# Sending the q transposes of four batches through the DMA crossbar instead of TensorE, and issuing the next batch's loads after the stores

## The chip, the cores and the metric

The kernel runs on one core of one Trainium2 chip. The time is the device time of one execution in microseconds (us); lower is better. Engines are named as the profile names them: PE is TensorE's matrix multiplication and PEld its weight loads, DVE is VectorE, ACT is ScalarE, POOL is GpSimd, SP is the engine that issues most of the DMA transfers. A transfer that an engine has issued runs on the 16 DMA engines, and is waited for by semaphore.

## The reference: what is computed

Sliding window attention for 8 batches of 8 heads, 576 positions and 64 elements a head, followed by a layer norm and a two-layer MLP with a residual. All inputs and the output are float32.

```python
# q, k, v: (8, 8, 576, 64); window = 64
scores = matmul(q, k.transpose(0, 1, 3, 2)) / sqrt(64)
rel = pos[:, None] - pos[None, :]
scores = where((rel >= 0) & (rel < window), scores, -1e9)
attn = softmax(scores, axis=-1)
x = matmul(attn, v)                        # heads side by side: (8, 576, 512)
xn = (x - mean(x)) / sqrt(var(x) + 1e-6) * g_ln
out = x + relu(xn @ w_ch1) @ w_ch2         # 512 -> 2048 -> 512
```

## The kernel before, in words

Positions 0 to 511 of a batch are one group of 512 tokens; the 64 last positions of all eight batches (the tails) make a ninth group. The outer loop, `for g in range(NGRP)`, runs the MLP of group `g`. While it does so, the same turn of the loop also carries the attention of group `g + 1` and the preparation of q, k and v of batch `g + 2`. In this text a turn is one pass of that loop.

The order of the work is written out by hand. `mlp_units` returns the MLP as a list of units, 30 of them from `g` = 2 on: 16 calls of `l1` (one 128 wide slice of the hidden layer, four 512 column matmuls, `hps`, and a relu on ScalarE into `hrT`), and then 14 calls of `stage`, two for each of seven products of a Strassen-like second layer (banks `pA`, `pB`, `pC`). `at(i, f, ...)` puts a step into slot `i`, which is emitted after unit `i`; a slot number that is too large means the last slot, after the last unit. Every engine, and every DMA queue, works through its own instructions in the order in which they were emitted. A step that waits therefore holds up what was emitted behind it on the same engine.

Slots 17 to 28 of a turn hold the preparation of batch `n = g + 2`, and these are the steps that matter here:

- `load_qk` (line 82) lets SP load q and k in two halves, each one transfer of 512 KB; from batch 2 on, each partition receives four successive positions, so that a run is 1 KB. `load_v` (line 135) loads v in four transfers of 256 KB. Loads of batch `n + 1` stand in slots 17, 18 and 23 of the turn before the one that casts them. Turn 1 loads batch 4 in slots 25, 26 and 28.
- `cast_qk` (line 120) converts a half of q and then the same half of k to float16 on GpSimd (line 126), in slots 11 and 16. GpSimd also carries `z_step` (line 306), the normalisation of a block of 128 tokens of group `g + 1`, in slots 2, 7, 12 and 17.
- `t_main` (line 211) brings a half of q or k into the layout with the head's elements on the partitions: eight 128x128 transposes on TensorE (line 216) into a PSUM tile `tp`, and one copy of 128x1024 into `qkT`, on ScalarE in these turns (line 207). The copy also puts the positions back into order. There are four such steps per batch, in slots 17 (q, first half), 19 (k, first half), 21 (q, second half) and 25 (k, second half).
- `s_mm` (line 240) computes the scores of two windows of 64 positions: 16 matmuls (line 263), with k as the weights and 64 columns of q as the moving operand, into two PSUM tiles `sc`; then two Exp instructions (line 266) on ScalarE write the float16 tile `pt`. `s_mm` of block 0 of batch `n` stands in slot 27, blocks 1 to 3 follow in slots 2, 7 and 12 of the next turn. `s_mask` (line 268) multiplies by the mask on VectorE.
- `b_step` (line 275) multiplies by v on TensorE (`xps`) and normalises on VectorE (line 297) into `x_norm`, a pool of four buffers of two blocks each; `z_step` follows it, and `zt_step` (line 321) transposes `z` on TensorE (line 328, tile `ztp`), six slots after the `b_step`.
- `stage` adds the second layer's products to `x_norm` and stores it: blocks 2 and 3 first, then blocks 0 and 1, at the end of the turn.
- `load_tail` (line 97) loads q, k and v of two batches' tails in six transfers, in slot 5 of turns 2, 4 and 6.

The transposes' PSUM tiles alternate between two banks (`t_tile`) up to slot 20 and share one after that.

Of the kernel before, what the change touches and what calls it, by code (L numbers as in the profile page):

```python
# [10 lines left out]
FP32 = mybir.dt.float32  # L11
# [3 lines left out]
AF = mybir.ActivationFunctionType  # L15
# [5 lines left out]
def kernel(  # L21
# [10 lines left out]
    nc = tc.nc  # L32
    B, H, S, D = q.shape
    DM = H * D
    HID = 4 * DM
    SM = 512
    NGRP = B + 1
    NKC = DM // 128
    NHC = HID // 128
    NHP = H // 2  # L40
    EPS = 1e-6
    scale = 1.0 / (D ** 0.5)

    p_const = ctx.enter_context(tc.tile_pool(name="pconst", bufs=1))
# [5 lines left out]
    p_xn = ctx.enter_context(tc.tile_pool(name="pxn", bufs=4))  # L50
# [21 lines left out]
    def t_tile(shape, name):  # L72
        i = 0 if tbank["shared"] else tbank["n"] % 2
        tbank["n"] = i + 1
        return ps_t.tile(shape, FP16, tag=f"t{i}", name=name)
# [3 lines left out]
    qkT, vA, vB, pts = {}, {}, {}, {}  # L79
    x_norm, zT, mvg, zsd, rstd = {}, {}, {}, {}, {}  # L80
# [36 lines left out]
        nc.gpsimd.tensor_copy(out=k16, in_=tk)  # L117
        nc.gpsimd.tensor_copy(out=vt[:, :, :, 0:D], in_=tv)

    def cast_qk(b, half):  # L120
        for x in range(2):
            t = qk32.pop((b, x, half))
            dst = p_in.tile([128, 8, 2, D], FP16, tag=f"qk16_{x}", name=f"qk16_{x}_{b}_{half}")
            qk16[(b, x, half)] = dst
            j = 2 if b < 2 else 4
            nc.gpsimd.tensor_copy(  # L126
                out=dst[:, :].rearrange("p (a j) e d -> p a e j d", j=j),
                in_=t[:, :].rearrange("p (a e j d) -> p a e j d", e=2, j=j, d=D),
            )
# [71 lines left out]
    def alloc_qkT(b):  # L201
        qkT[b] = [p_qkt.tile([128, NHP, SM + 64 * x], FP16, tag=f"qkT{x}", name=f"qkT{x}_{b}") for x in range(2)]
        nc.gpsimd.memset(qkT[b][1][:, :, 0:64], 0.0)

    def evac(x, out, in_):
        if x == 0:
            nc.scalar.copy(out=out, in_=in_)  # L207
        else:
            nc.vector.tensor_copy(out=out, in_=in_)

    def t_main(b, x, half, eng=None):
        src = qk16.pop((b, x, half))
        j = 2 if b < 2 else 4
        tp = t_tile([128, 8, 128], f"tp_{b}_{x}_{half}")
        for i in range(8):
            nc.tensor.transpose(out=tp[:, i, :], in_=src[:, i], identity=ident16)  # L216
        if b < 2:
            c0 = 64 * x + 256 * half
            dst = qkT[b][x][:, :, c0:c0 + 256]
        else:  # L220
            dst = qkT[b][x][:, 2 * half:2 * half + 2, 64 * x:64 * x + 512]
        evac(x if eng is None else eng, dst.rearrange("c h (p j) -> c h p j", j=j),
             tp[:, :].rearrange("c (h j) p -> c h p j", j=j))
# [16 lines left out]
    def s_mm(g, j, pe_mask=False):  # L240
        sc = [ps_s.tile([128, NHP, 2, 64], FP32, tag="sc", name=f"sc_{g}_{j}_{par}") for par in range(2)]
        pt = p_pt.tile([128, 2, NHP, 2, 64], FP16, tag="pt", name=f"pt_{g}_{j}")
        pts[(g, j)] = pt
        if pe_mask:
            m = mbias[:, :]
            mb = bass.AP(tensor=m.tensor, offset=m.offset, ap=[m.ap[0], [0, NHP * 2], m.ap[1]])
            for par in range(2):
                nc.tensor.matmul(
                    out=sc[par][:, :].rearrange("p h w i -> p (h w) i"), lhsT=ident16, rhs=mb,
                    start=True, stop=False, skip_group_check=True,  # L250
                )
        for hp in range(NHP):
            for iw in range(2):
                for par in range(2):
                    rows = slice(64 * par, 64 * par + 64)
                    if g == NGRP - 1:
                        lhsT = tailT[j][1][rows, iw, hp, :]
                        rhs = tailT[j][0][rows, hp, 64 * iw:64 * iw + 64]
                    else:
                        w = 2 * j + iw  # L260
                        lhsT = qkT[g][1][rows, hp, 64 * w:64 * w + 128]
                        rhs = qkT[g][0][rows, hp, 64 * w:64 * w + 64]
                    nc.tensor.matmul(out=sc[par][:, hp, iw, :], lhsT=lhsT, rhs=rhs,  # L263
                                     start=not pe_mask, stop=True, skip_group_check=pe_mask)
        for par in range(2):
            nc.scalar.activation(out=pt[:, par], in_=sc[par], func=AF.Exp, bias=0.0, scale=scale)  # L266

    def s_mask(g, j):
        pt = pts[(g, j)]
# [5 lines left out]
    def b_step(g, kb):  # L275
        kblk = f"{g}_{kb}"
        sfx, nb = ("r", 2) if g == NGRP - 1 else ("", None)
        if kb % 2 == 0:
            x_norm[(g, kb // 2)] = p_xn.tile([128, 2, DM], FP32, tag="xn" + sfx, name=f"xn_{g}_{kb // 2}", bufs=nb)
        xv = x_norm[(g, kb // 2)][:, kb % 2, :]  # L280
        xn = xv.rearrange("p (h d) -> p h d", h=H)
        xps = ps_x.tile([128, H, 128], FP32, tag="xps", name=f"xps_{kblk}")
        pt = pts.pop((g, kb))
        for h in range(H):
            par, hp = h % 2, h // 2
            for r in range(2):
                if sfx:
                    rhs = vT[kb][:, r, h, :]
                else:
                    rhs = (vA if r else vB)[g][:, kb, h, :]  # L290
                nc.tensor.matmul(out=xps[64 * r:64 * r + 64, h, :D + 1], lhsT=pt[:, par, hp, r, :], rhs=rhs,  # L291
                                 start=True, stop=True)
        rcp = p_blk.tile([128, H], FP32, tag="rcp", name=f"rcp_{kblk}")
        nc.vector.reciprocal(out=rcp, in_=xps[:, :, D])  # L294
        rcp_b = bass.AP(tensor=rcp.tensor, offset=rcp[:, :].offset,
                        ap=[rcp[:, :].ap[0], rcp[:, :].ap[1], [0, D]])
        nc.vector.tensor_tensor(out=xn, in0=xps[:, :, 0:D], in1=rcp_b, op=ALU.mult)  # L297
        stats = p_blk.tile([128, nc.vector.BN_STATS_DIM], FP32, tag="stats", name=f"stats_{kblk}")
        nc.vector.bn_stats(out=stats, in_=xv)  # L299
        if g not in mvg:  # L300
            mvg[g] = p_grp.tile([128, 4, 2], FP32, tag="mvg" + sfx, name=f"mvg_{g}", bufs=1 if sfx else 2)
        nc.vector.bn_aggr(out=mvg[g][:, kb, :], in_=stats)  # L302
        if g < 2:
            z_step(g, kb)
# [16 lines left out]
    def zt_step(g, kb, eng="act"):  # L321
        z = zsd.pop((g, kb))
        if g not in zT:
            sfx = "r" if g == NGRP - 1 else ""
            zT[g] = p_grp.tile([128, NKC, 512], FP16, tag="zT" + sfx, name=f"zT_{g}", bufs=1 if sfx else 2)
        ztp = t_tile([128, NKC, 128], f"ztp_{g}_{kb}")
        for kc in range(NKC):
            nc.tensor.transpose(out=ztp[:, kc, :], in_=z[:, 128 * kc:128 * (kc + 1)], identity=ident16)  # L328
        dst = zT[g][:, :, 128 * kb:128 * kb + 128]
        if eng == "act":  # L330
            nc.scalar.copy(out=dst, in_=ztp)  # L331
        else:
            nc.vector.tensor_copy(out=dst, in_=ztp)
# [208 lines left out]
    for i in range(8):  # L542
# [7 lines left out]
        out=mask[0:64], in_=mask[0:64], compare_op=ALU.is_gt, fill=0.0,  # L550
# [3 lines left out]
        out=mask[64:128], in_=mask[64:128], compare_op=ALU.is_ge, fill=0.0,  # L554
# [82 lines left out]
    for g in range(NGRP):  # L637
# [3 lines left out]
        def at(i, f, *a):  # L641
            slots[min(i, len(slots) - 1)].append((f, a))

        b = g + 1
# [26 lines left out]
        if g == 1:  # L671
# [39 lines left out]
            at(31, s_mask, 3, 0)  # L711
            for i, (x, half) in zip((21, 24, 25, 28), ((0, 0), (1, 0), (0, 1), (1, 1))):
                at(i, t_main, 3, x, half, 0)
            at(25, load_qk, 4, 0)
            at(26, load_qk, 4, 1)
            at(28, load_v, 4, 0, 4)
        if g == 2:
            at(3, w2_sums, 1, 0, 4)
            at(4, w2_sums, 1, 4, 8)
        if g > 1 and g + 2 < B:  # L720
            at(11, alloc_qkT, g + 2)
            at(11, cast_qk, g + 2, 0)
        if g > 1 and b < B:
            for j in range(4):
                if j:
# [11 lines left out]
            at(ts[3], zt_step, NGRP - 1, i)  # L737
        n = g + 2
        if g > 1 and n < B:
            at(16, cast_qk, n, 1)  # L740
            at(20, alloc_v, n)
            at(20, cast_v, n, 0, 2)
            at(21, cast_v, n, 2, 4)
            at(21, alloc_vB, n)
            at(21, make_vB, n)
            for i, (x, half) in zip((17, 19, 21, 25), ((0, 0), (1, 0), (0, 1), (1, 1))):
                at(i, t_main, n, x, half, 0)
            at(27, s_mm, n, 0)
            at(28, s_mask, n, 0)
            if n + 1 < B:  # L750
                at(17, load_qk, n + 1, 0)
                at(18, load_qk, n + 1, 1)
                at(23, load_v, n + 1, 0, 4)
        if g > 1:
            for i in range(1, 5):
                at(7 + i, s_sums, 0, 4, i)
# [1 line left out]
                at((15, 15, 19, 21)[i - 1], s_sums, 6, 8, i)  # L758
        for n, i in enumerate(TAILS.get(g + 1, ())):
            if n == 0:  # L760
                at(5, load_tail, i)
                at(24, cast_tail, i)
                at(27, t_tail, i, 0)
                at(29, t_tail, i, 1)
            else:
                at(25, load_tail, i)
# [40 lines left out]
```

The softmax here doesn't subtract the row's maximum and nothing guards it: scores larger than these inputs give would overflow.

## Time and profile before

| | |
|---|---|
| median of 13 runs | 324.89 us (324.37 to 326.11) |
| the profiled execution's own time | 326.11 us |
| its span in the profile | 324.4 us |
| TensorE busy | 310.2 us (96%) |
| VectorE, ScalarE, GpSimd busy | 205.6, 176.8, 163.5 us |
| transposes of q and k (`tp`, line 216) | 256 instructions, 20.1 us busy |
| moved by DMA | 51.08 MB, mean 157 GB/s |

The span is the time between the first and the last instruction that the profiler recorded. A line of the group tables reads: source line, engine, operation, output tile and input tiles, shapes and count; then the total busy time and the mean duration of one instruction; then the idle time of the engine just before these instructions and what ended it. Matmuls are pipelined, so that the duration of one is longer than the distance to the next: the price of a group on TensorE is read from the starts in the timeline.

### The profile page before, as it was taken

How to read it: one execution, taken by the hardware profiler on the slowest of the kernel's cores; microseconds unless marked ns; L12 is line 12 of the kernel's file. 1: busy time of each engine (PE TensorE's matmuls, PEld its weight loads, DVE VectorE, ACT ScalarE, POOL GpSimd, SP SyncE). 2: the span in 40 equal slices, each digit the busy share in tenths (PEclk: the TensorE clock that was granted, in tenths of full speed). 3: DMA queues.
4: the chain of work that ended last, by engine and by line, in shares of the span. 5: the costliest groups of instructions: out<-in, count | busy, mean ns of one | idle time of the engine just before them, and what ended most of it. 6: DMA issues, size and time to landing. Idle time of an engine off the chain costs nothing.

```text
span 324.4 us, 7813 instructions
## 1 busy us (share of the span) xinstructions
PE 310.2 (96%) x3229; PEld 204.6 (63%) x3229; DVE 205.6 (63%) x388; ACT 176.8 (54%) x292; POOL 163.5 (50%) x251
## 2 busy tenths in 40 slices
PE   6998998999998999999999999999999999999993
PEld 4566444597553479646964696558755965684582
DVE  1796755478793795499556954896459644751643
ACT  1586623487455764776548646774487157405600
POOL 7578756421991598169804982598127506200000
PEclk9999999999999999999999999999999999999998
DMA  8999999986179946904499359100480090003013
GB/s 191 281 384 258 351 311 269 279 276 131 36 237 258 208 134 190 257 3 129 146 260 208 125 153 242 62 2 2 153 199 2 22 266 6 2 2 130 0 35 97
DMA packets 85638, 51.08 MB, mean 157 GB/s; under 512 B 55681, under 2 KB 76673, under 8 KB 85602
## 3 DMA queue, kind: packets, MB, share of 16 engines
q1 hardware_dynamic: 84816, 48.11, 55.2%
q0 software_dynamic: 640, 2.33, 2.9%
q8 instruction: 25, 0.41, 0.5%
q10 hardware_dynamic: 146, 0.13, 0.1%
q14 instruction: 11, 0.09, 0.1%
HBM read 38.80 MB, written 9.44 MB: 149 GB/s over the span
## 4 chain that ended last, share of the span: by engine, by line
PE 77%; DMA 9%; POOL 5%; SPq 3%; DVE 2%; issue 1%; ACT 1%; POOLq 0%; ACTq 0%
PE hps L363 31%; PE pA L435 11%; PE pC L435 8%; PE pB L435 8%; PE hph L484 4%; DMA qk<-in_q_dram 4%; DMA w2s<-in_moe_w_ch_dram 3%; PE xps L291 3%; PE tp L216 3%; PE sc L263 3%; PE ch L375 3%; PE ztp L328 2%; SPq L139 2%; DMA w1s<-in_moe_w_ch_dram 2%; SPq L87 1%
## 5 line engine op out<-in xcount | busy, mean ns | idle before, releaser
L363 PE MATMUL hps<-zT,w1g 128*128 128x512 f16 x480 | 112.0, 380 | 0.0
L367 ACT ACTIVATE hrT<-hps 128x512 f16<-128x512 f32 x120 | 71.9, 599 | 35.2 <-PE hps L363 31.6
L363 PEld LDWEIGHTS <-w1g 128*128 128x128 f16 x480 | 44.1, 98 | 47.0 <-issue 1.0
L316 POOL TENSOR_SCALAR rsz<-mvg 128x1 f32<-128x1 f32 x28 | 12.2, 437 | 77.7 <-DVE mvg L302 77.0
L266 ACT ACTIVATE pt<-sc 128x512 f16<-128x512 f32 x72 | 39.0, 595 | 15.3 <-PE sc L263 13.8
L435 PEld LDWEIGHTS <-sS 128*128 128x128 f16 x448 | 42.9, 98 | 4.8
L207 ACT COPY qkT<-tp 128x1024 f16<-128x1024 f16 x26 | 26.2, 1012 | 34.5 <-PE tp L216 32.8
L126 POOL CAST qk<-qk 128x1024 f16<-128x1024 f32 x32 | 33.5, 1065 | 9.2 <-DMA qk<-in_q_dram 4.6
L331 ACT COPY zT<-ztp 128x512 f16<-128x512 f16 x36 | 21.1, 586 | 27.9 <-PE ztp L328 27.4
L442 DVE TENSOR_TENSOR xn<-pA,xn 128x512 f32<-128x512 f32 x28 | 19.2, 685 | 26.3 <-PE pA L435 22.9
L435 PEld LDWEIGHTS <-hrT 128*128 128x128 f16 x336 | 32.2, 98 | 5.0
L294 DVE RECIPROCAL rcp<-xps 128x8 f32<-128x8 f32 x36 | 7.4, 205 | 35.6 <-PE xps L291 35.2
L414 DVE TENSOR_TENSOR sS<-hrT 128x512 f16<-128x512 f16 (+1 forms) x42 | 21.4, 510 | 10.2 <-ACT hrT L367 10.2
L435 PE MATMUL pA<-wT,sS 128*128 128x256 f16 x224 | 26.9, 273 | 0.0
L435 PE MATMUL pC<-w2s,sS 128*128 128x256 f16 x224 | 26.8, 273 | 0.0
L297 DVE TENSOR_TENSOR xn<-xps,rcp 128x512 f32<-128x512 f32 x36 | 24.9, 691 | 2.8 <-DMA out_dram<-xn 1.6
L273 DVE TENSOR_TENSOR pt<-pt,mask 128x1024 f16<-128x1024 f16 x28 | 21.1, 761 | 8.6 <-ACT pt L266 8.5
L299 DVE BATCH_NORM_STATS2 stats<-xn 128x6 f32<-128x512 f32 x36 | 25.0, 695 | 1.2
L484 PE MATMUL hph<-zT,w1g 128*128 128x256 f16 x192 | 23.2, 273 | 1.8 <-ACT zT L331 1.1
L319 POOL TENSOR_SCALAR z<-xn,rsz 128x512 f16<-128x512 f32 x28 | 23.3, 833 | 2.9
L375 PE MATMUL ch<-w2s,hrT 128*128 128x512 f16 x96 | 23.7, 380 | 0.3 <-DVE xn L385 0.3
L484 PEld LDWEIGHTS <-w1g 128*128 128x128 f16 x192 | 18.2, 98 | 4.6 <-issue 1.9
(85 smaller groups left out, 438.9 us busy)
## 6 DMA issues: line engine op xcount, KB each, us to landing
out_dram<-xn SPq DMA_DIRECT2D x34, 256.0 KB, 3.6
qk<-in_q_dram SPq DMA_DIRECT2D x16, 512.0 KB, 4.7
qk<-in_k_dram SPq DMA_DIRECT2D x16, 512.0 KB, 5.9
v<-in_v_dram SPq DMA_DIRECT2D x32, 256.0 KB, 6.4
w2s<-in_moe_w_ch_dram SPq DMA_DIRECT2D x12, 512.0 KB, 6.1
w1s<-in_moe_w_ch_dram SPq DMA_DIRECT2D x4, 512.0 KB, 6.7
tk<-in_k_dram SPq DMA_DIRECT2D x8, 256.0 KB, 4.5
tv<-in_v_dram SPq DMA_DIRECT2D x8, 256.0 KB, 4.8
```

The lines of the kernel that those rows point to most:

```text
L126: nc.gpsimd.tensor_copy(out=dst[:, :].rearrange("p (a j) e d -> p a e j d", j=j), in_=t[:, :].rearrange("p (a e j d) -> p a e j d", e=2, j ...
L207: nc.scalar.copy(out=out, in_=in_)
L266: nc.scalar.activation(out=pt[:, par], in_=sc[par], func=AF.Exp, bias=0.0, scale=scale)
L297: nc.vector.tensor_tensor(out=xn, in0=xps[:, :, 0:D], in1=rcp_b, op=ALU.mult)
L299: nc.vector.bn_stats(out=stats, in_=xv)
L319: nc.gpsimd.tensor_scalar(out=z, in0=xv, scalar1=rs, scalar2=nm, op0=ALU.mult, op1=ALU.add)
L363: nc.tensor.matmul(out=hps, lhsT=w1g[:, kc, 128 * hc:128 * (hc + 1)], rhs=zT[g][:, kc, :], start=(kc == 0), stop=(kc == NKC - 1),)
L367: nc.scalar.activation(out=hrT[:, hc, :], in_=hps, func=AF.Relu, bias=0.0, scale=1.0)
L375: nc.tensor.matmul(out=ch[kb], lhsT=hrT[:, hc, 128 * kb:128 * (kb + 1)], rhs=w2s[:, hc, :], start=(hc == 0), stop=(hc == NHC - 1),)
L414: nc.vector.tensor_tensor(out=o, in0=x, in1=y, op=op)
L435: nc.tensor.matmul(out=bank[which][:, p, :], lhsT=a[:, c, 128 * p:128 * p + 128], rhs=wv[:, c, :], start=(first and p == 0 and c == 0), st ...
L484: nc.tensor.matmul(out=hps[:, e], lhsT=w1g[:, kc, 128 * hc:128 * (hc + 1)], rhs=zT[g][:, kc, 256 * half:256 * half + 256], start=(kc == 0) ...
```

## The change

Three things change. First, for batches 4 to 7 (`XQ = 4`), `t_main` of q is no longer eight TensorE transposes and a copy, but one DMA transpose that SP issues, from the float16 q tile straight into `qkT`. Transposes of k stay on TensorE. [...] Second, the casts and transposes of these batches are reordered: both halves of q are cast in slot 11 and transposed in slot 13, the first half of k is cast in slot 11 after them, and k is transposed in slots 17 and 21. Third, `load_qk` and `load_v` of the next batch go to the last slot of a turn, behind the stores, and `load_tail` goes from slot 5 to slot 1. The two `x_norm` tiles of groups 4 and 5 are also taken from their pool in the other order. A second switch, `XZ = 99`, would send the transposes of `z` the same way, and is off.

```diff
+    XQ = 4
+    XZ = 99
...
-    def cast_qk(b, half):
-        for x in range(2):
+    def cast_qk(b, half, xs=(0, 1)):
+        for x in xs:
...
+    def flat(b):
+        return qkT[b][0][:, :, :].rearrange("p h m -> p (h m)")
...
         src = qk16.pop((b, x, half))
+        if b >= XQ and x == 0:
+            dst = flat(b)[:, 2 * SM * half:2 * SM * half + 2 * SM]
+            nc.sync.dma_start_transpose(out=dst.rearrange("p (a t) -> p a t", t=128),
+                                        in_=src[:, :].rearrange("p a e d -> p (a e d)"))
+            return
...
                         rhs = qkT[g][0][rows, hp, 64 * w:64 * w + 64]
+                        if g >= XQ:
+                            qb = flat(g)[rows, SM * hp + 16 * w:SM * hp + 16 * w + 16]
+                            rhs = bass.AP(tensor=qb.tensor, offset=qb.offset, ap=[qb.ap[0], [128, 4], [1, 16]])
...
-            nc.scalar.activation(out=pt[:, par], in_=sc[par], func=AF.Exp, bias=0.0, scale=scale)
+            o, i = pt[:, par], sc[par][:, :]
+            if XQ <= g < NGRP - 1:
+                o = o.rearrange("p h w (r j) -> p (h w) r j", j=4)
+                i = i.rearrange("p h w (j r) -> p (h w) r j", j=4)
+            nc.scalar.activation(out=o, in_=i, func=AF.Exp, bias=0.0, scale=scale)
...
-            x_norm[(g, kb // 2)] = p_xn.tile([128, 2, DM], FP32, tag="xn" + sfx, name=f"xn_{g}_{kb // 2}", bufs=nb)
+            if (g, kb // 2) not in x_norm:
+                for h in ((1, 0) if g // 2 == 2 else (0, 1)):
+                    x_norm[(g, h)] = p_xn.tile([128, 2, DM], FP32, tag="xn" + sfx, name=f"xn_{g}_{h}", bufs=nb)
...
-            at(25, load_qk, 4, 0)
-            at(26, load_qk, 4, 1)
-            at(28, load_v, 4, 0, 4)
+            at(40, load_qk, 4, 0)
+            at(40, load_qk, 4, 1)
+            at(40, load_v, 4, 0, 4)
...
-            at(11, cast_qk, g + 2, 0)
+            if g + 2 >= XQ:
+                at(11, cast_qk, g + 2, 0, (0,))
+                at(11, cast_qk, g + 2, 1, (0,))
+                at(11, cast_qk, g + 2, 0, (1,))
+            else:
+                at(11, cast_qk, g + 2, 0)
...
-            at(16, cast_qk, n, 1)
+            at(16, cast_qk, n, 1, (1,) if n >= XQ else (0, 1))
...
-            for i, (x, half) in zip((17, 19, 21, 25), ((0, 0), (1, 0), (0, 1), (1, 1))):
+            for i, (x, half) in zip((13, 17, 13, 21) if n >= XQ else (17, 19, 21, 25),
+                                    ((0, 0), (1, 0), (0, 1), (1, 1))):
...
-                at(17, load_qk, n + 1, 0)
-                at(18, load_qk, n + 1, 1)
-                at(23, load_v, n + 1, 0, 4)
+                at(40, load_qk, n + 1, 0)
+                at(40, load_qk, n + 1, 1)
+                at(40, load_v, n + 1, 0, 4)
...
-                at(5, load_tail, i)
+                at(1, load_tail, i)
```

More of the change, by code (lines that the diff above doesn't have):

```diff
@@ L325, in zt_step @@
             zT[g] = p_grp.tile([128, NKC, 512], FP16, tag="zT" + sfx, name=f"zT_{g}", bufs=1 if sfx else 2)
+        if XZ <= g < NGRP - 1:
+            nc.sync.dma_start_transpose(out=zT[g][:, :, 128 * kb:128 * kb + 128], in_=z)
+            return
         ztp = t_tile([128, NKC, 128], f"ztp_{g}_{kb}")
```

## The prediction

> **What bounds the kernel now.** I read the page's busy times first, then busy times by stretch, then the order of TensorE and GpSimd in one stretch, last the transfers.
>
> The page's first part, share of the span in brackets:
>
> ```profile
> PE 310.2 (96%) x3229; PEld 204.6 (63%) x3229; DVE 205.6 (63%) x388; ACT 176.8 (54%) x292; POOL 163.5 (50%) x251
> ```
>
> Busy time in stretches that I chose. Those from 100.4 us on are one turn each of the loop over `g` (`g` = 2, 3, 4, 5):
>
> ```profile
> core 0: us, PE busy (x) PEld busy (x) DVE busy (x) ACT busy (x) POOL busy (x), PEclk, DMA share, GB/s
> 100.40:133.36 32.96, 32.96 (x378) 22.71 (x369) 23.59 (x44) 21.26 (x35) 20.94 (x31) 1.00 0.83 189
> 133.36:166.83 33.47, 33.47 (x392) 22.78 (x390) 23.30 (x45) 21.99 (x36) 20.10 (x31) 1.00 0.53 139
> 166.83:199.66 32.83, 32.83 (x365) 22.63 (x364) 21.91 (x41) 20.23 (x33) 20.61 (x31) 1.00 0.75 184
> 199.66:233.00 33.34, 33.34 (x389) 22.68 (x388) 23.15 (x46) 21.99 (x36) 20.10 (x31) 1.00 0.22 60
> ```
>
> In these turns TensorE is never idle, at a granted clock of 1.00. Every instruction taken from it there shortens the run by its own slot, until somebody else is late. The transposes that the change removes (batches 4 to 7) all lie in these four turns.
>
> TensorE in order of time, the second half of the turn `g` = 2 (start, duration):
>
> ```profile
> 119.52 0.62 PE L216 MATMUL tp<-ident,qk 128*128 128x128 f16 x8
> 119.98 1.04 PE L435 MATMUL pB<-w2s,hrT 128*128 128x256 f16 x8
> 120.85 0.39 PE L328 MATMUL ztp<-ident,z 128*128 128x128 f16 x4
> 121.07 1.04 PE L435 MATMUL pB<-w2s,hrT 128*128 128x256 f16 x8
> 121.95 0.61 PE L216 MATMUL tp<-ident,qk 128*128 128x128 f16 x8
> 122.39 1.91 PE L435 MATMUL pA<-wT,sS 128*128 128x256 f16 x16
> ...
> 130.59 0.41 PE L263 MATMUL sc<-qkT,qkT 64*128 64x64 f16 x16
> 130.93 0.29 PE L232 MATMUL tpq<-ident,tq 128*128 128x128 f16 x2
> ```
>
> The printed duration runs to the modelled end of the last result; what a group costs is the distance between starts. Eight transposes: 122.39 - 121.95 = 0.44 us; the next two groups give 124.59 - 124.14 = 0.45 and 128.75 - 128.30 = 0.45. (The same is the 20.1 us for 256 instructions of that group on the page, 79 ns each, with the joints.) Scores of one step (16 matmuls): 130.93 - 130.59 = 0.34.
>
> **The change, part by part.** *Removed from TensorE.* Two groups of eight transposes per turn (q, two halves), four turns: 8 x 0.445 = 3.56 us, all on the path. Their 8 evacuations on ScalarE (1.01 us each) go too; TensorE's list of waits has no row for them, so they count for nothing.
>
> *The k groups move* from slots 19 and 25 to 17 and 21, same count and price. GpSimd has to have cast k in time: the first k half is now the third cast of slot 11.
>
> GpSimd in the same turn:
>
> ```profile
> 114.71 2.02 POOL L126 CAST qk<-qk 128x1024 f16<-128x1024 f32 x2
> 116.82 0.51 POOL L316 TENSOR_SCALAR rsz<-mvg 128x1 f32<-128x1 f32 x1
> 117.41 0.61 POOL L317 TENSOR_TENSOR rsz<-rsz,mhalf 128x1 f32<-128x1 f32 x1
> 118.11 0.67 POOL L318 TENSOR_SCALAR rsz<-mvg,rsz 128x1 f32<-128x1 f32 x1
> 118.89 0.82 POOL L319 TENSOR_SCALAR z<-xn,rsz 128x512 f16<-128x512 f32 x1
> ```
>
> Three casts end at 114.71 + 3 x 1.01 = 117.75; TensorE wants k at 119.5. Covered by 1.8 us. But behind the casts on the same engine stands the normalisation of block 2, whose `z` ends at 119.71 and is transposed at 120.85. A third cast ahead of it moves it to 120.72, and its weight load takes 0.1 us before the matmul: the margin of 1.14 us is spent to about zero. In the turns 3 and 5 the same two rows stand 1.36 us apart, in turn 4 1.14. I take 0.1 us of new wait in turns 2 and 4, 0.2 in all. Ends: 0, and a whole cast in each turn, 4 x 1.01 = 4.0 us, if GpSimd comes later to slot 11. Block 3's `z` is not touched: GpSimd waits there for VectorE (0.60 us idle) and the cast moved away from slot 16 makes room.
>
> *Loads behind the stores.* Per turn 4 loads of q and k (512 KB) and 4 of v (256 KB) are issued by SP after the turn's last stores instead of at slots 17 to 23, for turns 1 to 4; the six tail loads (1.25 MB) follow at slot 1 instead of 5 where there are any (turns 2, 4, 6). They are needed later than before by nobody, but they start some 20 us later. In turn 3 the last stores are issued at 135.4. The queue's rows are 0.4 to 0.6 us per q or k load, so all four are out by 138; with the stores that is about 2.6 MB, and the stretch from 92 to 100 us, full of loads, moved 314 to 323 GB/s: landed at about 144. GpSimd casts at 148.5. Covered by 4 us. In turn 2 (stores at 101.5, landed by 110, casts at 114.7) as well. The v loads (1.1 to 1.8 us of SP each) land by 150, wanted at 158. Price 0. Stores no longer stand behind loads, but TensorE waits for no store; the new order of the two x buffers removes up to 1.6 us of VectorE's wait for `out`, which TensorE doesn't see either: 0.
>
> *Scores.* Their moving operand is now read as four runs of 16 elements. No row shows so short a run. 512 columns take 0.87 / 4 = 0.217 us, 0.42 ns a column; 16 matmuls of 64 columns, two row halves at once, would need 0.22 us of streaming, and take 0.34. So reading may be 1.57 times slower at no cost; at twice slower it is 0.43 - 0.34 = 0.09 us in each of 16 steps, 1.5 us. I take 0, the contiguous row being nearest. No gain is possible there, the matmuls are the same in number.
>
> *Exp* (32 instructions) reads PSUM with a step. The nearest rows are ScalarE's copies, the first with a step of 128 elements, the second contiguous:
>
> ```profile
> L207 ACT COPY qkT<-tp 128x1024 f16<-128x1024 f16 x26 | 26.2, 1012 | 34.5 <-PE tp L216 32.8 <-POOL rsz L316 1.6
> L207 ACT COPY tkT<-tpk 128x1024 f16<-128x1024 f16 x4 | 4.0, 1012 | 3.5 <-PE tpk L237 3.5
> ```
>
> Same price, so 0. If each cost 0.6 us more, 19 us of ScalarE work would lie in turns where it has 11 us free each: still covered, but for the odd late relu, 2 us at most by my estimate.
>
> *The crossbar transposes*, the thing that the trace doesn't show. Two transfers of 256 KB per turn from SP, after the two q casts. Wanted by the scores at slot 27. In turns 3 and 5 SP can issue the first at 149.5 and the second at 150.6; the scores stand at 164.8, or 163.9 after the gain: 13 us for the pair. In turns 2 and 4, SP first issues v loads (7.1 us before) and tail loads (5.0): it is free at about 116, as the casts end at 116.8; but some 4.6 MB queued since 101.2 at about 250 GB/s keep the DMA engines until about 119.5, which leaves 10 us to 129.7. Rows for a 256 KB transfer within SBUF or near it:
>
> ```profile
> v<-in_v_dram SPq DMA_DIRECT2D x32, 256.0 KB, 6.4
> vB<-vA POOLq DMA_DIRECT2D x5, 260.0 KB, 4.8
> vB<-vA POOLq DMA_DIRECT2D x5, 195.0 KB, 6.6
> ```
>
> These are latencies, and a pair overlaps: 5 to 9 us. Hidden, price 0, margin 1 to 8 us. The far end: the page's main queue moved 84816 packets in 55.2% of 16 engines' 324.4 us, 34 ns a packet. At that pace 10 us hold 16 x 10000 / 34 = 4700 packets, or 110 bytes each for a pair. If the crossbar works in smaller pieces, it is late. With 64 byte pieces a pair takes 17 us, 4 to 7 us late in four turns, 22 us in all; that is my upper end.
>
> The Trainium skill speaks against this edit: "VectorE: DVE Perf Modes", section "Rules for kernel authors", advises TensorE for a 128x128 transpose if PSUM is an acceptable destination, and its section "The three transpose paths" gives 1309 ns for one through the DMA crossbar. No run here shows a crossbar transpose yet. If eight such blocks followed each other, an estimate from that figure is 10.5 us per transfer and 21 us a pair, and the sum would be some 30 us worse than mine. The trace's 0.45 us for eight on TensorE is what makes its rule dear here, as TensorE is the engine without a gap.
>
> **Sum.** -3.56 + 0.2 = -3.36 us. The profiled execution took 326.11 us, a span of 324.4 and 1.7 around it; it is the slowest of the 13 shown, 1.2 above their median. Off the median: 324.89 - 3.36 = 321.5.
>
> **Rivals.** *The crossbar is late* (slower). The pair lands after the scores want it. It decides from 0.9 us of lateness per turn, since 4 x 0.89 is the gain: a pair longer than 11 us in turns 2 and 4 and 14 in turns 3 and 5. Against it the SBUF rows above, for it that no row is a transpose. Price at the upper end: 321.5 + 22 = 343; just over the point, at pairs of 14 us (4 us late in two turns, 1 in the others), 321.5 + 10 = 331; at 12 us, 325.5.
> *GpSimd becomes the bound of block 2.* A whole cast of wait in each turn: 321.3 + 4.0 = 325.3, no change. For it the margin of 1.14 us against 1.01; against it that GpSimd runs through from 111 to 122 us in this trace without waiting for a load. Half of it: 323.3.
> *Scores or Exp pay for the short runs*: 321.5 + 1.5 to 3.5 = 323 to 325.
>
> **How the numbers follow.** Forecast as it stands, 0.60, own range 320.8 to 322.6 (wait of 0 to 1.3 us, gain of 0.44 to 0.55 a group). GpSimd or short runs in part, 0.14, of it 0.09 still faster, 0.05 within 0.2% (about what a measurement of this kernel can tell). Crossbar late, 0.20: 0.01 within, 0.19 slower, a third of it under 328. Whole stalls elsewhere, 0.06 slower. Together faster 0.69, same 0.06, slower 0.25. The range runs from 320.4 (a group worth 0.55 and no wait) to 328, which leaves out the larger part of the late crossbar.
>
> **What would show it.** Right: TensorE still busy through the four turns, each about 0.85 us shorter, `tp` at 24 groups instead of 32, no wait of `sc` for a DMA, the transposes landing within 9 us of issue. Wrong: a wait of `sc` for `qkT` at slot 27; `ztp` waiting for `z` by 0.5 us or more; 16 score matmuls above 0.34 us; Exp above 595 ns; a cast waiting for q or k from memory in turns 2 to 5.

## The result, and the profile after

The changed kernel takes 322.29 us (median of 11 runs, 321.08 to 324.07), the kernel before 325.2 (48 runs by then): a ratio of 0.9904, 95% interval 0.9889 to 0.992, about 3.1 us less. The forecast was 3.4 us less, 321.5 us. An execution that took over 1.5% longer than the fastest of its kernel is left out of the ratios; that is one each of the runs `xbar_only`, `combo` and `dummy8` below.

The profiled execution took 322.02 us, with a span of 319.6. That is 4.8 us less than the span before, but only a part belongs to the change. Busy time by stretch, each stretch from the first `hps` of a turn to that of the next:

```profile
core 0: us, PE busy (x) PEld busy (x) DVE busy (x) ACT busy (x) POOL busy (x), PEclk, DMA share, GB/s
98.88:131.06 32.18, 32.12 (x354) 21.68 (x349) 23.41 (x44) 19.23 (x33) 21.00 (x31) 1.00 0.80 186
131.06:163.48 32.42, 32.42 (x376) 21.72 (x373) 23.20 (x45) 19.97 (x34) 20.14 (x31) 1.00 0.58 155
163.48:195.65 32.17, 32.12 (x351) 21.68 (x349) 21.85 (x42) 18.20 (x31) 20.67 (x31) 1.00 0.87 211
195.65:228.06 32.41, 32.41 (x375) 21.72 (x373) 23.15 (x45) 19.97 (x34) 20.15 (x31) 1.00 0.66 154
```

Turns 2 to 5 took 32.85, 33.30, 32.83 and 33.31 us before, by the same marks. They lose 0.67, 0.88, 0.66 and 0.90 us, 3.11 in all. The remaining 1.6 us of the span lie ahead of turn 2, which begins at 98.88 instead of 100.51 us. That start moves from run to run: in the experiments below, most of which leave that part of the program as it is, it lies anywhere from 98.5 to 101.2. Lengths of turns are therefore compared here, not spans.

TensorE in the second half of turn 2, and the GpSimd instructions that matter for it (start, duration):

```profile
117.89 0.62 PE L226 MATMUL tp<-ident,qk 128*128 128x128 f16 x8
118.35 1.04 PE L457 MATMUL pB<-w2s,hrT 128*128 128x256 f16 x8
119.44 0.40 PE L350 MATMUL ztp<-ident,z 128*128 128x128 f16 x4
...
128.30 0.41 PE L276 MATMUL sc<-qkT,qkT 64*128 64x64 f16 x16
128.64 0.40 PE L242 MATMUL tpq<-ident,tq 128*128 128x128 f16 x4
```

```profile
113.08 3.46 POOL L128 CAST qk<-qk 128x1024 f16<-128x1024 f32 x3
...
118.44 0.94 POOL L338 TENSOR_SCALAR z<-xn,rsz 128x512 f16<-128x512 f32 x1
```

The `ztp` group starts 1.09 us after the `pB` group ahead of it; before it was 0.87 (119.98 to 120.85). These 0.22 us are a wait for `z`: its normalisation ends at 119.38, behind three casts that take 3.46 us. Scores take 128.64 - 128.30 = 0.34 us as before, and start without a wait for q. No cast of these turns waits for a load either: between 98 and 230 us GpSimd waits only for VectorE.

The transfers, from the page's third part and the issues with their size and time to landing:

```profile
q1 hardware_dynamic: 93264, 50.21, 60.0%
```

```profile
vB<-vA POOLq DMA_DIRECT2D x5, 260.0 KB, 2.9
qkT<-qk SPq DMA_TRANSPOSE x8, 3.2
```

A crossbar transpose of 256 KB lands 3.2 us after its issue, and holds SP for 1.26 us in the median (2.70 at most). The queue has 93264 - 84816 = 8448 packets and 2.1 MB more than before: 1056 packets of some 249 bytes for each of the eight. Its time rises from 0.552 x 16 x 324.4 = 2865 to 0.600 x 16 x 319.6 = 3068 engine microseconds, 25 for a transpose, which is 1.6 us on sixteen engines. This is a rough estimate, as other transfers change too: by the shares of `k_late` (58.8% of 319.9 us) and `xbar_only` (61.2% of 321.4 us), which move the same packets, it would be 18 or 35, that is 1.1 or 2.2 us. So the rival of a late crossbar needed pieces of less than 110 bytes, and they are more than twice that.

### The profile page after: what moved, and what is told of

Its sections match the earlier page's. It is cut to its first block, busy times and chain, and to the rows that moved or that the text cites. A ratio compares the mean times of both kernels' runs of the same rounds, so it can differ in the third digit from the quotient of the medians.

```text
span 319.6 us, 7692 instructions
## 1 busy us (share of the span) xinstructions
PE 306.7 (96%) x3165; PEld 200.6 (63%) x3165; DVE 202.9 (63%) x388; ACT 168.7 (53%) x284; POOL 164.2 (51%) x251
## 3 DMA queue, kind: packets, MB, share of 16 engines
q1 hardware_dynamic: 93264, 50.21, 60.0%
## 4 chain that ended last, share of the span: by engine, by line
PE 72%; POOL 10%; DMA 10%; SPq 3%; issue 2%; DVE 1%; ACT 1%; POOLq 0%; ACTq 0%
PE hps L385 28%; PE pA L457 10%; PE pC L457 8%; PE pB L457 7%; PE hph L506 5%; DMA qk<-in_q_dram 4%; DMA w2s<-in_moe_w_ch_dram 4%; POOL qk L128 3%; PE xps L310 3%; PE ch L397 3%; PE sc L276 3%; PE ztp L350 2%; SPq L141 2%; DMA w1s<-in_moe_w_ch_dram 2%; PE tp L226 2%
## 5 line engine op out<-in xcount | busy, mean ns | idle before, releaser
L335 POOL TENSOR_SCALAR rsz<-mvg 128x1 f32<-128x1 f32 x28 | 11.2, 399 | 73.6 <-DVE mvg L321 72.9
L457 PEld LDWEIGHTS <-sS 128*128 128x128 f16 x448 | 43.1, 98 | 4.9
L128 POOL CAST qk<-qk 128x1024 f16<-128x1024 f32 x32 | 34.5, 1095 | 8.6 <-DMA qk<-in_q_dram 3.9
L212 ACT COPY qkT<-tp 128x1024 f16<-128x1024 f16 x18 | 18.1, 1012 | 29.5 <-PE tp L226 29.5
L436 DVE TENSOR_TENSOR sS<-hrT 128x512 f16<-128x512 f16 (+1 forms) x42 | 25.0, 596 | 10.2 <-ACT hrT L389 10.2
```

Of the source, the lines that this page charges most:

```text
L128: nc.gpsimd.tensor_copy(out=dst[:, :].rearrange("p (a j) e d -> p a e j d", j=j), in_=t[:, :].rearrange("p (a e j d) -> p a e j d", e=2, j ...
L436: nc.vector.tensor_tensor(out=o, in0=x, in1=y, op=op)
L457: nc.tensor.matmul(out=bank[which][:, p, :], lhsT=a[:, c, 128 * p:128 * p + 128], rhs=wv[:, c, :], start=(first and p == 0 and c == 0), st ...
```

## The experiments

Lengths of turns in us, from the first `hps` of one to that of the next, and the ratio to the kernel before with its 95% interval:

| run | turn 2 | 3 | 4 | 5 | ratio |
|---|---|---|---|---|---|
| before | 32.85 | 33.30 | 32.83 | 33.31 | |
| changed | 32.18 | 32.42 | 32.17 | 32.41 | 0.9904 (0.9889 to 0.992) |
| loads_only | 32.84 | 33.31 | 32.82 | 33.31 | 0.9991 (0.9976 to 1.0005) |
| xbar_only | 32.19 | 33.18 | 32.48 | 33.22 | 0.9966 (0.995 to 0.9981) |
| v_last | 32.19 | 32.42 | 32.17 | 32.41 | 0.9908 (0.9883 to 0.9933) |
| noswap | 32.19 | 32.42 | 32.16 | 32.42 | 0.9911 (0.9884 to 0.9937) |
| k_late | 31.95 | 32.42 | 31.94 | 32.41 | 0.9895 (0.9877 to 0.9912) |
| xq3 | 32.18 | 32.43 | 32.17 | 32.42 | 0.9931 (0.9908 to 0.9955) |
| xz4 | 32.18 | 31.53 | 32.16 | 31.52 | 0.9815 (0.9795 to 0.9835) |
| combo | 31.95 | 33.06 | 31.16 | 31.53 | 0.9861 (0.9821 to 0.9901) |
| xz4_klate | 31.95 | 31.52 | 31.68 | 31.52 | 0.9797 (0.9772 to 0.9822) |

All edits are made to the changed kernel. The lengths of turns come from one profiled execution of each run.

### Each part alone

```diff
-    XQ = 4
+    XQ = 99
```

> XQ = 99: no q goes through the crossbar, all casts, transposes and scores are as before; only the loads stand behind the stores and load_tail in slot 1. Theory (TensorE's slots alone set the gain, loads are covered): the time of the kernel before, 325.2 us within 0.5, turns 2 to 5 of 32.85, 33.30, 32.83 and 33.31 us as before. Rival (half of the gain or more comes from moving the loads, by less contention in turn 1 or at a turn's end): 323.7 or less. Rival (late loads cost something that the crossbar's gain hides): 326 or more, with a cast waiting for q or k.

Measured: 324.48 us, ratio 0.9991, turns as before to 0.01 us. Moving the loads alone is worth nothing, as the theory had it.

```diff
-            at(40, load_qk, 4, 0)
-            at(40, load_qk, 4, 1)
-            at(40, load_v, 4, 0, 4)
+            at(25, load_qk, 4, 0)
+            at(26, load_qk, 4, 1)
+            at(28, load_v, 4, 0, 4)
...
-                at(40, load_qk, n + 1, 0)
-                at(40, load_qk, n + 1, 1)
-                at(40, load_v, n + 1, 0, 4)
+                at(17, load_qk, n + 1, 0)
+                at(18, load_qk, n + 1, 1)
+                at(23, load_v, n + 1, 0, 4)
...
-                at(1, load_tail, i)
+                at(5, load_tail, i)
```

> The crossbar for q as in the changed kernel, but the loads back in slots 17, 18 and 23 (25, 26, 28 in turn 1) and load_tail in slot 5. Theory: the same as the changed kernel, 322.1 us within 0.5, as TensorE loses the same eight groups, and waits of 0.2 us for block 2's z in turns 2 and 4. Rival (the loads had to move, because they collide with the crossbar transposes or hold them up in SP's queue): sc waits for qkT by a few us in some turns, 324 us or more.

Measured: 323.97 us, ratio 0.9966. Here the theory falls: the crossbar alone keeps 1.1 of 3.1 us. But it isn't the rival's wait either. In the list of waits `sc` never waits for `qkT`. Against the changed kernel, turns 3 and 5 are 0.8 us longer each, turn 4 is 0.3. Turn 3 begins with these rows on VectorE, and with this one on TensorE:

```profile
134.58 0.21 DVE L313 RECIPROCAL rcp<-xps 128x8 f32<-128x8 f32 x1 [3.18 <-PE xps L310]
136.02 0.69 DVE L316 TENSOR_TENSOR xn<-xps,rcp 128x512 f32<-128x512 f32 x1 [1.23 <-DMA out_dram<-xn]
136.75 0.69 DVE L318 BATCH_NORM_STATS2 stats<-xn 128x6 f32<-128x512 f32 x1
137.47 0.18 DVE L321 BATCH_NORM_AGGREGATE mvg<-stats 128x2 f32<-128x6 f32 x1
137.57 0.66 DVE L290 TENSOR_TENSOR pt<-pt,mask 128x1024 f16<-128x1024 f16 x1
```

```profile
138.29 0.45 PE L310 MATMUL xps<-vt,pt 128*64 128x65 f16 x16 [0.69 <-POOL rsz L335]
```

VectorE waits 1.23 us for a store: the buffer that it is about to overwrite has not gone out. The mask stands behind it in VectorE's queue and ends at 138.23, and TensorE's `xps`, which needs the masked tile, starts at 138.29 after 0.69 us of idling. (The row names an instruction of GpSimd that ends at 138.29, too, but writes nothing that `xps` reads. The weight loads of the same group, which read the masked tile, are shown waiting 1.2 us for the mask.) The changed kernel's VectorE has this instead, with no wait ahead of line 316:

```profile
134.69 0.21 DVE L313 RECIPROCAL rcp<-xps 128x8 f32<-128x8 f32 x1 [3.17 <-PE xps L310]
134.93 0.69 DVE L316 TENSOR_TENSOR xn<-xps,rcp 128x512 f32<-128x512 f32 x1
```

At the end of turn 2, SP's queue in that run and, below it, in the changed kernel says why the stores are late:

```profile
125.34 4.47 SPq L141 DMA_DIRECT2D v<-in_v_dram  x4
129.91 4.39 SPq L423 DMA_DIRECT2D out_dram<-xn  x4
```

```profile
129.56 2.78 SPq L423 DMA_DIRECT2D out_dram<-xn  x4
```

SP issues the v loads until 129.8, and only then the first store: 1.05 us before turn 3 starts (130.96), where the changed kernel has it 1.50 us before (131.06). Then the four stores hold SP for 4.39 us instead of 2.78, and land 4.5 us after their issue in the median instead of 2.2:

```profile
out_dram<-xn SPq DMA_DIRECT2D x4, 256.0 KB, 4.5
```

```profile
out_dram<-xn SPq DMA_DIRECT2D x4, 256.0 KB, 2.2
```

Between 129 and 133 us the main queue's packets fill 107% of the DMA engines' time here, and 51% in the changed kernel. In the kernel before the v loads also stood in front of the stores, and VectorE waited 1.6 us in three places, but the mask was still in time. Is it the loads of v, or those of q and k?

```diff
-            at(40, load_qk, 4, 0)
-            at(40, load_qk, 4, 1)
+            at(25, load_qk, 4, 0)
+            at(26, load_qk, 4, 1)
...
-                at(40, load_qk, n + 1, 0)
-                at(40, load_qk, n + 1, 1)
+                at(17, load_qk, n + 1, 0)
+                at(18, load_qk, n + 1, 1)
```

> Between the changed kernel and the run with the loads in their old slots: q and k are loaded in slots 17 and 18 again (25 and 26 in turn 1), only the four v loads of 1.1 us of SP each stay behind the stores; load_tail in slot 1. Theory (with the loads in their old slots it is v's place in SP's queue, directly ahead of the stores, that makes VectorE wait for the store of the x_norm buffer and TensorE for VectorE): no wait of VectorE for out, turns 3 and 5 at 32.42 us instead of 33.2, turn 4 at 32.17, 322.1 us. Rival (traffic of the q and k loads beside the crossbar transposes, or before the stores, is what costs): turns 3 and 5 stay near 33.2, 323.9 us.

Measured: 321.85 us, the turns of the changed kernel to 0.01 us, no wait of VectorE for `out`. SP at the end of turn 2, with the stores in front:

```profile
129.78 2.78 SPq L423 DMA_DIRECT2D out_dram<-xn  x4
132.65 3.26 SPq L141 DMA_DIRECT2D v<-in_v_dram  x4
```

The q and k loads may stand where they were. Of these loads, only v's four had to move. Two things stay open. Moving them takes away both their place ahead of the stores and their traffic beside them, and no run separates the two. And `load_tail` stands in slot 1 here, in slot 5 in `xbar_only`; there the tails' loads are issued by 108.3 and 173.6 us, long before TensorE's waits in turns 3 and 5 (138.3 and 204.0), but for the 0.3 us of turn 4 they are not ruled out.

```diff
-                for h in ((1, 0) if g // 2 == 2 else (0, 1)):
+                for h in (0, 1):
```

> The changed kernel with the x_norm tiles of groups 4 and 5 taken in the old order, so that block 0 of group 4 overwrites the half of group 2 that is stored last. Theory (stores that lead the queue land at 134.2 to 134.6, VectorE writes at 134.9): no wait or up to 0.3 us on VectorE, none on TensorE, 322.1 us. Rival (the swap is what keeps VectorE and TensorE free at a turn's start): xps waits 0.7 us in turns 3 and 4 or more, 323.5 us.

Measured: 322.49 us, the same turns. With the stores in front, the order of the two `x_norm` tiles makes no difference to the turns; whether it would with the v loads in front was not tried.

### The wait for z

```diff
-                at(11, cast_qk, g + 2, 0, (1,))
...
+            if n >= XQ:
+                at(16, cast_qk, n, 0, (1,))
...
-            for i, (x, half) in zip((13, 17, 13, 21) if n >= XQ else (17, 19, 21, 25),
+            for i, (x, half) in zip((13, 19, 13, 21) if n >= XQ else (17, 19, 21, 25),
```

> The first half of k is cast in slot 16 (behind block 2's z on GpSimd) instead of slot 11, and transposed in slot 19 instead of 17. Theory (the third cast ahead of z is what made TensorE wait 0.22 us in turns 2 and 4): both waits go, turns 2 and 4 fall from 32.18 to 31.96 us, 0.44 us less in all, 321.7 us where the changed kernel has 322.1. Rival (the missing 0.4 us is something else, for example the changed order of TensorE's groups): turns 2 and 4 stay at 32.18. A new wait of tp for k in slot 19 would cost up to 0.5 us a turn.

Measured: 321.89 us, turns 2 and 4 at 31.95 and 31.94. TensorE in turn 2:

```profile
118.64 1.05 PE L457 MATMUL pB<-w2s,hrT 128*128 128x256 f16 x8
119.52 0.39 PE L350 MATMUL ztp<-ident,z 128*128 128x128 f16 x4
```

The distance is 0.88 us again. Both waits were the third cast, 0.46 us of turns in all. In the total time this is too little to show: the two intervals overlap.

### Where a group taken from TensorE pays nothing

```diff
-    XQ = 4
+    XQ = 3
```

> XQ = 3: q of batch 3 goes through the crossbar as well, so turn 1 of TensorE loses two groups of transposes (0.89 us). Rival A (every group taken from TensorE pays): 321.2 us where the changed kernel has 322.1. Theory (a group pays only where TensorE is the one that ends last; at the end of turn 1 TensorE waits 1.4 us for GpSimd's z, so the time moves into that wait): 322.1 within 0.4, the wait of ztp for z grows from 1.4 to about 2.2 us. Rival B (the DMA queue is full in turn 1, sc waits for qkT): slower.

Measured: 322.54 us. From its first `hph` to the first `hps` of turn 2, turn 1 lasts 39.84 us in the kernel before, in the changed one and in this one, though TensorE has two groups less to do here. At its end, in the changed kernel and in this run:

```profile
97.35 0.40 PE L350 MATMUL ztp<-ident,z 128*128 128x128 f16 x4 [1.37 <-POOL z L338]
```

```profile
99.64 0.40 PE L350 MATMUL ztp<-ident,z 128*128 128x128 f16 x4 [1.89 <-POOL z L338]
```

TensorE is busy for 36.90 us of this turn instead of 37.73. The wait for GpSimd grows by 0.52 us, and a new wait of `xps` for the mask takes 0.31: together the 0.83 us. So here the wait for `z` ends the turn, and work taken from TensorE only lengthens its waits. Whether the ratio, somewhat above the changed kernel's, is more than its later start (turn 2 at 101.17) is left open: the two intervals overlap.

### How much the crossbar may grow

```diff
+            scr = done32[(b, half)][:, :].bitcast(FP16)
+            for i in range(4):
+                part = scr[:, 1024 * (i % 2):1024 * (i % 2) + 1024]
+                nc.sync.dma_start_transpose(out=part.rearrange("p (a t) -> p a t", t=128),
+                                            in_=src[:, :].rearrange("p a e d -> p (a e d)"))
```

(`done32` is the float32 tile that q's half was cast from.)

> Ahead of each q transpose SP issues four more of the same size into float32 staging memory that is free by then; the output is the same. By the changed kernel's rows (1.26 us of SP each, 3.2 us from issue to landing, the third waiting for the first's landing) the second real one lands some 16 us after the first issue instead of 4 to 6. Theory (the pair is hidden by a margin of 4 to 6 us in turns 2 and 4 and 8 to 9 in turns 3 and 5): sc waits about 6 us in turns 2 and 4 and 2 in turns 3 and 5, about 337 us. Rival (the transposes also slow the engines or other transfers, so that margins are not all there is): well above 340. Rival (they overlap in the DMA engines and the margin is larger): under 330.

Measured: 363.44 us, ratio 1.1164 (1.1127 to 1.1201), on the side of the first rival. The wait of `sc` is there, but far dearer than the theory had it. SP in turn 2, its wait for extra transposes to land (in the four turns together), the list of TensorE's waits, and busy times around the first wait:

```profile
117.33 6.69 SPq L225 DMA_TRANSPOSE qk<-qk  x4
124.12 2.08 SPq L227 DMA_TRANSPOSE qkT<-qk  x1
126.30 12.04 SPq L225 DMA_TRANSPOSE qk<-qk  x4
138.38 1.32 SPq L227 DMA_TRANSPOSE qkT<-qk  x1
```

```profile
SPq L225 <- DMA qk<-qk: 12.4, 10, 4.1
```

```profile
PE sc L283 <- DMA qkT<-qk: 35.4, 5, 12.9
```

```profile
128.50:131.50 3.00, 0.28 (x9) 0.18 (x9) 1.12 (x2) 0.00 (x0) 1.27 (x2) 0.96 1.19 118
131.50:141.60 10.10, 0.00 (x0) 0.00 (x0) 0.00 (x0) 0.00 (x0) 0.00 (x0) 0.50 0.95 149
141.60:145.00 3.40, 3.36 (x25) 2.54 (x25) 0.69 (x1) 1.56 (x3) 0.00 (x0) 0.51 0.19 73
145.00:148.00 3.00, 3.00 (x38) 1.77 (x37) 0.69 (x1) 1.78 (x3) 0.00 (x0) 1.00 0.31 107
```

Ten transposes keep SP from 117.3 to 139.7, 2.2 us each instead of the 1.26 that I had reckoned with. That is not the price of issuing one: taken one by one the ten take 1.3 us in the median, 17.0 in all (the longest 3.9). In the rest SP waits, most of it for landings: the extra transposes write to the two halves of one tile in turn, so that a later one waits until an earlier one has landed, up to 4.1 us. That part of the delay is made by the experiment. Its longest piece falls into the second group of four, which takes 12 us while `vB`'s two transfers run as well. The first half's real transpose is in time; the second keeps the scores waiting for 12.9 us.

TensorE's waits add up to 35.4 us of the 43.1 that the span is longer than the changed kernel's. Most of the rest is the clock: it falls to 0.50 some 3 us into the wait, and stays at 0.51 for 3.4 us after it, which is work at half speed. After the three other waits above 5 us it is 0.50 for some 3.5 us, too; half of four times 3.5 is 7 us, by estimate. "TensorE: Matmul & The Clock Gate" of the Trainium skill, in its part on the clock gate, has the clock halved after an idle window of some 3.4 us and full again after as much work; the rows agree.

### More of the same

```diff
-    XZ = 99
+    XZ = 4
```

> XZ = 4: the transposes of z of groups 4 to 7 go through the crossbar as well, 16 more transfers of 128 KB from SP in turns 3 to 6. Theory (each group taken from TensorE pays its own slot while nobody else is late): 16 groups of four transposes at 0.22 us (120.85 to 121.07 in the kernel before) are 3.5 us, 318.6 us; TensorE no longer waits for z in turn 4. Rival (the crossbar or SP's queue becomes late: hps at a turn's start waits for zT, or sc for qkT): less than half of that, or slower.

Measured: 318.95 us, ratio 0.9815. Turns 3 and 5 each lose another 0.89 us, turn 6 goes from 30.60 to 29.71, which is four groups of 0.22 each time. Turn 4 gains nothing. SP there, and TensorE at its end:

```profile
176.10 1.15 SPq L106 DMA_DIRECT2D tq<-in_q_dram  x1
...
180.50 1.12 SPq L108 DMA_DIRECT2D tv<-in_v_dram  x1
181.79 4.41 SPq L346 DMA_TRANSPOSE zT<-z  x2
186.30 2.63 SPq L220 DMA_TRANSPOSE qkT<-qk  x2
189.02 2.54 SPq L346 DMA_TRANSPOSE zT<-z  x2
```

```profile
192.43 0.40 PE L242 MATMUL tpq<-ident,tq 128*128 128x128 f16 x4 [0.32 <-POOL tq L118]
195.59 1.67 PE L385 MATMUL hps<-zT,w1g 128*128 128x512 f16 x7 [0.58 <-DVE xn L464]
```

The tails' loads go first, and the transposes of `z`, whose first block was ready at 171, start at 181.8. The last is issued at 190.34 and lands 5.2 us later, at about 195.5. The next turn's first `hps`, which reads `zT`, starts at 195.59, after 0.58 us of idling. (The row names VectorE, which finished at 195.48; which of the two held it isn't shown.) With the 0.32 us for the tail's cast this is 0.90 us, as much as four groups of `z` are worth.

```diff
     XZ = 4, and the casts and slots of k as in the run k_late
...
             if n == 0:
-                at(1, load_tail, i)
+                if g == 2:
+                    at(1, load_tail, i)
...
+        if g in (3, 5):
+            at(14, load_tail, TAILS[g + 2][0])
```

> XZ = 4 and the first k half cast in slot 16, and the tails of turns 4 and 6 loaded one turn earlier, in slot 14 of turns 3 and 5, so that SP reaches the transposes of turn 4 some 6 us sooner. Theory (in turn 4 of the run with XZ = 4 the z transposes stood behind the tail loads on SP, and that took back 1.1 us): turn 4 falls from 32.16 to about 31.1 us, turn 2 from 32.18 to 31.95, together 317.7 us or less. Rival (the tail loads now hold up turns 3 and 5): these rise from 31.53, no gain over 318.95.

Measured: 321.26 us, ratio 0.9861 (317.79 to 322.49 in five runs; why they spread so far isn't known). Turn 4 falls to 31.16 as expected, and turn 3 rises to 33.06, as the rival said. The tail loads now stand ahead of the last two `z` blocks there:

```profile
157.29 0.85 SPq L108 DMA_DIRECT2D tv<-in_v_dram  x1
158.24 4.66 SPq L346 DMA_TRANSPOSE zT<-z  x2
```

```profile
165.96 2.35 PE L385 MATMUL hps<-zT,w1g 128*128 128x512 f16 x10 [1.37 <-DMA zT<-z]
```

Turn 5, with the same order, loses nothing (31.53). There SP comes to the last two blocks 23.9 us after the turn's start instead of 25.3, and issues them in 3.61 us instead of 4.66. Why it gets there sooner was not settled.

The last run takes `XZ = 4` and the slots of `k_late`, and leaves the tails alone:

> XZ = 4 with the first k half cast in slot 16 and transposed in slot 19, tails as in the changed kernel. Theory: the turns of the run with XZ = 4 (31.53, 32.16, 31.52 and 29.71 us for turns 3 to 6), and turn 2 without its wait for z, 31.95 us: 0.2 us below that run, 318.7 us, 0.981 of the kernel before. Rival (k's cast after z delays the tail casts or k's transposes and takes more than that): above 319.2 us.

Measured: 318.21 us (317.86 to 318.97, 5 runs), ratio 0.9797, the lowest median, though its interval overlaps that of `xz4`. Turn 2 loses its wait, and turn 4 falls to 31.68, more than expected:

```profile
98.53:130.48 31.95, 31.95 (x354) 21.77 (x349) 23.00 (x44) 19.25 (x33) 21.00 (x31) 1.00 0.81 188
162.00:193.68 31.68, 31.23 (x335) 20.77 (x333) 22.46 (x42) 16.08 (x27) 20.42 (x31) 1.00 1.06 232
```

In turn 4 TensorE is still idle for 0.45 us, all of it ahead of `tpq`, for the tail's cast; the next turn's first `hps` no longer waits. The DMA engines are full (1.06).

## Why the prediction was right, point by point

**The eight groups.** The term of 3.56 us held: turns 3 and 5, which have no new wait, lose 0.88 and 0.90 us for two groups each, against 0.89. (The remark that the page's 79 ns for each of 256 instructions says the same is a wrong reading: eight times 79 ns is 0.63 us, the printed duration with its overlap. The price is the 0.445 us between starts.)

**The wait for z** was placed in the right turns and mis-sized: 0.2 us forecast, 0.44 measured (0.22 in each of turns 2 and 4). I took three casts at 1.01 us; they took 3.46 us together. The wait is a fifth of the whole cast that the GpSimd rival had as its price. The small loss explains the small error: -3.56 + 0.44 = -3.12 us against 3.11 in the turns and 0.96% of 325.2 = 3.12 in the times. (The own range was added up loosely: its terms give 320.5 to 322.7, not 320.8 to 322.6.)

**Loads behind the stores, price 0.** Right for the change as it stands, but by luck, for the reasoning is the step that failed. "TensorE waits for no store" was read from a trace in which that wait was covered. With q gone from TensorE each turn is up to 0.9 us shorter, the stores run into v's loads, and VectorE's wait gets through to TensorE by the mask. With v's loads in front turns 2 to 5 take 131.07 us together, with the stores in front 129.19: 1.9 us. I had listed the move of the loads as worth nothing because I priced it against the old length of the turn. The new order of the two `x_norm` tiles, which I had expected to remove VectorE's wait for `out`, isn't what removes it: with this order and v's loads in front the wait is 4.9 us, with the old order and the stores in front there is none.

**Scores and Exp, price 0.** Right: with q's positions left as they were loaded, a step's matmuls take 0.34 us in runs of 16 elements, and Exp 595 ns with a stepped read, both as before.

**The crossbar, hidden.** Right, with a margin. Landing takes 3.2 us in the median and 4.7 at most; in turn 2 the two are issued at 118.2 and 120.9, and the scores stand at 128.3. The 10.5 us for a transfer of eight blocks, which I had estimated from the 1309 ns in "VectorE: DVE Perf Modes" of the Trainium skill, do not hold for one instruction of eight blocks: the run shows 3.2. Nor does the page's advice to prefer TensorE where PSUM will do as the destination pay here, where TensorE is the engine that ends last: each group of eight was worth some 0.44 us. "DMA: Bandwidth & Descriptors", in "Latency and other measured facts", gives 261 GB/s for DMA transposes with a non-contiguous middle dimension and some 350 to 400 for contiguous ones, by estimate 1.0 or 0.7 us of all engines for 256 KB; the packet times here say 1.6, roughly. The rival of a late crossbar did not come about. Its mechanism exists, as the run with eight more transposes a turn shows, but not at the size of the change.

## What to carry to other kernels

Taking a step from the engine that ends last pays its slot, and shortens everybody else's time by as much: look at which covered waits have less margin than that, stores in a shared queue among them. Where the same step lies in a stage that another engine ends, it pays nothing, as in turn 1. A stored buffer that is soon overwritten should not have loads in front of its store in the same queue: here v's four loads in front of the stores cost 1.9 us.

## What I had not expected of the hardware

Stores issued right behind the v loads held SP for 4.39 us instead of 2.78 and took 4.5 us to land instead of 2.2. Three casts in a row on GpSimd took 3.46 us where two took 2.02; why is not shown. And TensorE's wait of 12.9 us is followed by 3.4 us at a granted clock of 0.51, so a late transfer costs more than its lateness.
